# Retention and two MoE layers on one core: half of the first token chunk moved into a short pass between the seven-product passes, clamp of weight words moved to VectorE

## The chip, the cores and the metric

The kernel runs on one core of a Trainium2 chip. The metric is the device time of one execution in microseconds. Five engines work side by side: TensorE (PE for its matmuls, PEld for its weight loads), VectorE (DVE), ScalarE (ACT), GpSimd (POOL), and SyncE (SP), which here issues all the DMAs. Each works through its own instructions in the order in which they were written into the program.

## What is computed

```python
def _attn_ref(q, k, v):            # 4 batches, 8 heads, 576 positions, 64 dims
    scores = scale * np.matmul(q, k.transpose(0, 1, 3, 2))
    Dmat = np.where(rel >= 0, gamma[:, None, None] ** rel[None, :, :], 0.0)
    return np.matmul(scores * Dmat, v)

def _moe_ref(x, w_gate, w_val, w_out):      # 2304 tokens, 512 wide, 1536 hidden
    g = x @ w_gate
    silu = g * (1.0 / (1.0 + np.exp(-g)))
    return silu * (x @ w_val) @ w_out

def _moe2_ref(x, w_in, w_out):              # 2048 hidden
    r = np.maximum(x @ w_in, 0.0)
    return (r * r) @ w_out
```

The output of the retention is `x` of the first layer, and the output of the first layer is `x` of the second. The weights of both layers arrive as 64-bit floating-point numbers and are made into 32-bit ones on the chip. The matmuls run on a pair of reduced-precision parts (`hi` and `lo`) of each operand: every product of two 32-bit operands is three matmuls (`three`, L312): hi by hi, hi by lo, lo by hi.

## The kernel before, in words

**Tiles.** The activations live in `xy`, a tile of 128 partitions by four channel blocks by 2304 tokens. The hidden width is cut into units of 128 rows: 12 of them (`F1`) in the first layer, 16 (`F2`) in the second. A weight *unit* is a 128x512 block: gate ("g"), value ("v") or output ("o") of one hidden block in the first layer, input ("i") or output ("o") in the second. That makes 36 units of the first layer and 32 of the second.

**Conversion of a unit** (`words` L163, driven by `conversion` L191 and `conversion2` L261). A DMA brings 512 KB of 64-bit words into a `raw` tile. Two ScalarE instructions take out the low bits and the magnitude, one instruction clamps the magnitude (L175, on GpSimd: `pool_e.tensor_scalar` with max and min), and three instructions of VectorE shift and mask, put the sign in, and add the low bits. The result is stored to DRAM (`wst`). For the first layer, `parts_unit` (L155) also makes the hi and lo parts at once (one ScalarE copy, one VectorE subtraction). The raw tiles come from a pool of two (`raw_p`), and for part of the time from places in `xy` that are not in use yet (`spare`). The generators yield between the steps; `pump` and `pump2` run so many steps between other pieces of work.

**Order of the work.** Four stages follow each other.

1. Retention, 16 pairs of heads in a loop of 18 turns (L510 on), with an order that is written by hand: while `chain["on"]` holds, each instruction is placed behind the one before it on its engine. In turns 6 to 17 each turn also does one projection of the *first chunk* (the first `M0` = 512 tokens): gate and value of the hidden units 0 to 5, four channel blocks by three matmuls. Fourteen units are converted alongside.
2. The rest of the first chunk (L777 to L805): the output matmuls `out0` (L352) of units 0 to 5, and gate, value and output of units 6 to 11, for which the other 22 units of the first layer are converted. All twelve output contributions add up in four PSUM banks, and the sum is then copied into `xy`. `renew` (L569) of the next pass and `build(0)` are interleaved with the last seven steps.
3. Two *seven-product passes* over the other 1792 tokens (L827 on). Each takes two blocks of 448 tokens; for a pair of hidden units the four block products of 2x2 blocks of weights and activations are made from seven products of sums and differences (Strassen's method in Winograd's form). A *system* is one pair of hidden units for gate or value: seven *slots* of six matmuls. `renew` makes the seven activation operands (four subtractions on GpSimd, then a hi and lo split on ScalarE and VectorE), `stationary` (L241) makes the weight operands on GpSimd with splits, in the first of the passes only; they are stored (`win`) and loaded again in the second. `out1` (L723) then does the output matmuls of the pair into a PSUM bank, and adds them to `xy`. The second layer's units are converted during these passes, with `PACE` steps per slot.
4. Three such passes over all 2304 tokens with blocks of 384 for the second layer, and the DMA of the output.

Outside the chained loop of stage 1 a planner orders the instructions: it goes through a simulated time line and takes, for each engine, the first instruction in program order that is ready then; so a step of a conversion that stands late in the program can be placed early where an engine is free, and how far ahead is limited by the raw tiles and the tiles that it writes.

The operands of a slot come from here:

```python
    ROWS = ((1, 2), (6, 3), (7, 4), (5,))          # which products share a weight tile
    for x in ((1, n), (7, n - 1), 0, (2, n), (4, n - 1), 1, (6, n), (3, n - 1), 2, (5, n)):
        # (i, k): slot i of system k;  0, 1, 2: a third of the due output tiles
```

Of the kernel before, what the change touches and what calls it, by code (L numbers as in the profile page):

```python
# [9 lines left out]
F32 = mybir.dt.float32  # L10
# [37 lines left out]
PUMPS = {0: 1, "E": 2, "out": 4}  # L48

PACE = (0.3, 1.9)  # L50
# [9 lines left out]
def retention_moe_kernel(  # L60
# [19 lines left out]
    raw_p = pool(ctx, "raw_p", 2)  # L80
    cv_p = pool(ctx, "cv_p", 1)
    ph1 = ExitStack()
    ctx.enter_context(ph1)
    xs_p = pool(ph1, "xs_p", 4)
    h_p = pool(ph1, "h_p", 2)
    t_p = pool(ph1, "t_p", 2)
    wa_p = pool(ph1, "wa_p", WA)
# [42 lines left out]
    def prefetch(upto):  # L130

        while loads["next"] <= min(upto, len(order) - 1):
# [11 lines left out]
            what, f = order[i]  # L144
            src = w1[f, :, "gvo".index(what), :].bitcast(U32)
# [4 lines left out]
    wst = {(1, *u): part_p.tile([P, 512], F32, tag=f"w1{u[0]}{u[1]}", name="wst") for u in order}  # L150
# [4 lines left out]
    def parts_unit(i):  # L155
        wf = w_t.pop(i).bitcast(F32)
        hi, lo = weight_tiles()
        act.copy(hi, wf)
        dve.tensor_tensor(out=lo, in0=wf, in1=f32(hi), op=ALU.subtract)
        sp.dma_start(out=wst[(1, *order[i])], in_=wf)  # L160
        units[order[i]] = (hi, lo)

    def words(raw, back, flat):  # L163
# [11 lines left out]
        pool_e.tensor_scalar(out=wf, in0=wf, scalar1=TINY, scalar2=HUGE, op0=ALU.max, op1=ALU.min)  # L175
# [15 lines left out]
    def conversion():  # L191
        for i in range(len(order)):
            prefetch(max(i, min(i + 3, loads["cap"])))
            raw, back = raw_t[i]
            for n, wt in enumerate(words(raw, back, raw_flat.pop(i, None))):
                w_t[i] = wt
                if n == 2:
                    if i:
                        parts_unit(i - 1)
                else:  # L200
                    yield
# [6 lines left out]
        parts_unit(len(order) - 1)  # L208
        yield


    seq2 = [(what, f) for f in range(F2) for what in "io"]
    wst.update({(2, *u): part_p.tile([P, 512], F32, tag=f"w2{u[0]}{u[1]}", name="wst") for u in seq2})
    raw2, free2, count = {}, [None, None], {"load2": 0}

    def load2(upto):
        while count["load2"] < len(seq2) and count["load2"] <= upto and free2:
            j = count["load2"]
            count["load2"] += 1
            back = free2.pop(0)  # L220
            flat = None
            if back is None:
                flat = raw_p.tile([P, 1024], U32, tag="raw", name="raw")
                raw = flat.rearrange("p (a n) -> p a n", a=2)
            else:
                raw = back.bitcast(U32)
            what, f = seq2[j]
            src = w2[f, :, "io".index(what), :].bitcast(U32)
            sp.dma_start(out=raw, in_=src.rearrange("p (a n) -> p a n", a=2))
            raw2[j] = raw, back, flat  # L230

    def give_back(j):
        back = raw2.pop(j)[1]
        if back is None or loads["open"]:
            free2.append(back)
# [25 lines left out]
    def conversion2():  # L261
        behind = None
        for j, u in enumerate(seq2):
            load2(j + 2)
            for n, wt in enumerate(words(*raw2[j])):
                if n == 3 and behind is not None:
                    sp.dma_start(out=behind[0], in_=behind[1])
                if n != 2:
                    yield
            give_back(j)  # L270
            behind = wst[(2, *u)], wt.bitcast(F32)
        sp.dma_start(out=behind[0], in_=behind[1])
        yield

    pumped = {"n": 0, "limit": 0}
    convert = conversion()
    convert2 = conversion2()

    def pump2(k=1):
        for _ in range(k):  # L280
            next(convert2, None)
# [7 lines left out]
    def ensure(key):  # L289
        while key not in units:  # L290
            next(convert)
            pumped["n"] += 1
# [28 lines left out]
    def project(f, what):  # L321
        ensure((what, f))
        ps, w = bank(what), units.pop((what, f))
        for cc in range(CC):
            three(ps, cut(w, cc * P, P), xs[cc], cc == 0, cc == CC - 1)
        return ps
# [3 lines left out]
    def hidden0(k):  # L330
# [11 lines left out]
        if f < HALF:  # L342
            hi, lo = weight_tiles()
        else:
            hi = h_p.tile([P, M0], F32R, tag="hh", name="h_hi")
            lo = h_p.tile([P, M0], F32R, tag="hl", name="h_lo")
# [3 lines left out]
    acc = []  # L350

    def out0(f):  # L352

        if f == 0:
            acc.extend(ps_a.tile([P, 512], F32, tag=f"a{i}", name=f"a{i}") for i in range(CC))
        ensure(("o", f))
        w, h = units.pop(("o", f)), hs.pop(f)
        for cc in range(CC):
            three(acc[cc], cut(w, cc * P, P), h, f == 0, f == F1 - 1)
        if f == F1 - 1:  # L360
            for cc, a in enumerate(acc):
# [553 lines left out]
```

## Time and profile before

| | us |
|---|---|
| median of three runs (lowest, highest) | 950.38 (950.35, 951.18) |
| the profiled execution | 946.6 |
| its span in the trace | 944.8 |
| busy: PE, PEld | 897.1, 780.6 |
| busy: DVE, ACT, POOL | 668.2, 435.8, 283.8 |

The span is the time from the first to the last instruction that the trace holds; what the execution's own time has beyond it lies around it. Busy time of PE is modelled: the end of a pipelined matmul is not recorded, so that two matmuls in flight overlap and a busy PE can still take fewer matmuls than it could. The number of matmuls in a stretch, (x...) in the views, tells more. Every instruction of this kernel is recorded at the line of the helper that issues it, so groups are told apart by the names of the tiles: `g`, `v`, `z` are PSUM tiles of projections, `oacc` of output matmuls, `a` of the first chunk's output; `xo` the activation operands and `wi` the weight operands of the seven products; `raw`, `w` the conversion; `w_hi`, `w_lo` split units.

### The profile page before, as it was taken

The page shows a single profiled execution, that of the slowest core. Times are in us where ns is not written, and L with a number is a line of the kernel's source. Part 1 is how long each engine was busy: PE and PEld are TensorE (multiplying, and loading weights), DVE is VectorE, ACT ScalarE, POOL GpSimd, SP SyncE. Part 2 cuts the span into 40 slices and gives each one's busy share as a digit, 9 for nine tenths or more (in the row PEclk, how much of TensorE's full clock was granted, in tenths as well). Part 3 has the DMA queues.
Part 4 walks back from the last instruction along what each step waited for, and adds up shares of the span by engine and source line. Part 5 has one row for each costly group of instructions (what it writes and reads, how often), then busy time and mean ns, then how long its engine had stood idle before and what let it go on. Part 6 is the DMA issues. An engine that isn't in the chain of part 4 may idle for free.

```text
span 944.8 us, 13815 instructions
## 1 busy us (share of the span) xinstructions
PE 897.1 (95%) x5050; PEld 780.6 (83%) x5050; DVE 668.2 (71%) x1011; ACT 435.8 (46%) x780; POOL 283.8 (30%) x207
## 2 busy tenths in 40 slices
PE   7899977777999999999999999999999999999998
PEld 6777745555899899799999998898989889989986
DVE  4777687778989999986545798767754557554553
ACT  3655645544775566635323545544423334243220
POOL 2544474565565653643000263310200002000000
PEclk9999989998999999999999999999999999999999
DMA  9988496653798889779445446455464544564402
GB/s 331 338 281 272 141 329 218 175 172 134 249 319 315 313 289 350 247 244 321 152 152 156 151 183 233 166 181 184 139 198 149 188 138 152 167 212 145 131 26 67
DMA packets 80660, 196.30 MB, mean 208 GB/s; under 512 B 8144, under 2 KB 18896, under 8 KB 80592
## 3 DMA queue, kind: packets, MB, share of 16 engines
q1 hardware_dynamic: 80592, 195.41, 61.9%
q8 instruction: 40, 0.66, 0.3%
q14 instruction: 28, 0.23, 0.1%
HBM read 136.14 MB, written 59.24 MB: 207 GB/s over the span
## 4 chain that ended last, share of the span: by engine, by line
PE 68%; DVE 11%; DMA 9%; issue 5%; POOL 3%; ACT 3%; SPq 0%; POOLq 0%; DVEq 0%; ACTq 0%
PE oacc L112 28%; PE g L112 19%; PE v L112 10%; DVE w L112 5%; PE z L112 5%; DMA raw<-in_w 4%; PE o L112 3%; PE s L112 2%; POOL w L112 2%; DMA xy<-in_w 2%; DVE wi L112 1%; DVE xy L112 1%; DMA qk_sb<-in_qk 1%; PE kvs L112 1%; DVE ho_lo L112 1%
## 5 line engine op out<-in xcount | busy, mean ns | idle before, releaser
L112 PE MATMUL g<-xo_h,wi 128*128 128x384 f32 (+1 forms) x768 | 232.1, 353 | 6.0 <-ACT cai L112 2.9
L112 POOL TENSOR_SCALAR w<-w 128x512 f32<-128x512 f32 x68 | 143.3, 2108 | 139.7 <-ACT w L112 123.3
L112 PE MATMUL oacc<-wo,ho_hi 128*128 128x512 f32 x576 | 181.8, 393 | 0.0
L112 PEld LDWEIGHTS g<-xo_h,wi 128*128 128x128 f32 x768 | 143.0, 188 | 17.4 <-ACT cai L112 3.6
L112 PE MATMUL g<-xo_l,wi 128*128 128x384 f32 (+1 forms) x384 | 135.1, 352 | 0.0
L112 PEld LDWEIGHTS oacc<-wo,ho_hi 128*128 128x128 f32 x576 | 107.6, 188 | 18.4
L112 PE MATMUL v<-xo_h,wi 128*128 128x448 f32 (+1 forms) x384 | 121.4, 355 | 1.3 <-DVE t L112 1.0
L112 PE MATMUL oacc<-ho_hi,wo 128*128 128x448 f32 x384 | 120.8, 366 | 0.0
L112 DVE TENSOR_TENSOR xy<-oacc,xy 128x448 f32<-128x448 f32 (+1 forms) x134 | 85.4, 644 | 39.7 <-PE oacc L112 39.4
L112 PE MATMUL oacc<-wo,ho_lo 128*128 128x512 f32 x288 | 113.4, 394 | 0.0
L112 POOL TENSOR_TENSOR xy<-xy 128x768 f32<-128x768 f32 (+1 forms) x20 | 44.0, 2212 | 160.9 <-DVE xo_l L112 160.6
L112 PEld LDWEIGHTS v<-xo_h,wi 128*128 128x128 f32 x384 | 72.2, 190 | 8.0 <-DVE t L112 1.4
L112 PEld LDWEIGHTS oacc<-ho_hi,wo 128*128 128x128 f32 x384 | 72.1, 188 | 6.3
L112 PEld LDWEIGHTS g<-xo_l,wi 128*128 128x128 f32 x384 | 72.2, 188 | 5.2
L112 PE MATMUL oacc<-ho_lo,wo 128*128 128x448 f32 x192 | 70.2, 366 | 0.0
L112 PE MATMUL v<-xo_l,wi 128*128 128x448 f32 (+1 forms) x192 | 67.8, 353 | 0.0
L112 ACT ACTIVATE raw<-raw 128x512 uint32<-128x512 uint16 x58 | 39.4, 680 | 58.8 <-DMA raw<-in_w 57.2
L112 DVE TENSOR_TENSOR wo<-wo 128x512 fp32r<-128x512 f32 x72 | 49.3, 703 | 22.7 <-ACT wo L112 22.6
L112 PE MATMUL z<-xo_h,wi 128*128 128x448 f32 (+1 forms) x192 | 60.3, 352 | 3.8 <-ACT xy L112 2.9
L112 PEld LDWEIGHTS oacc<-wo,ho_lo 128*128 128x128 f32 x288 | 54.0, 188 | 11.2
L112 ACT CAST wo<-wo 128x512 fp32r<-128x512 f32 x72 | 43.3, 620 | 34.2 <-DMA wo<-wst 33.4
L112 DVE TENSOR_SCALAR w<-w 128x512 uint32<-128x512 uint32 x68 | 44.0, 648 | 20.3 <-POOL w L112 20.0
(118 smaller groups left out, 1587.4 us busy)
## 6 DMA issues: line engine op xcount, KB each, us to landing
wi<-win SPq DMA_DIRECT2D x84, 512.0 KB, 3.7
win<-wi SPq DMA_DIRECT2D x60, 512.0 KB, 4.7
raw<-in_w SPq DMA_DIRECT2D x58, 512.0 KB, 4.5
wo<-wst SPq DMA_DIRECT2D x72, 256.0 KB, 4.3
wst<-w SPq DMA_DIRECT2D x68, 256.0 KB, 4.6
w_in<-wst SPq DMA_DIRECT2D x40, 256.0 KB, 4.9
qk_sb<-in_qk SPq DMA_DIRECT2D x15, 576.0 KB, 6.0
kv_sb<-in_kv SPq DMA_DIRECT2D x15, 576.0 KB, 4.7
```

Of the source, the lines that this page charges most:

```text
L112: i = op(*args, **kw)
```

## The change

The first chunk is made shorter, 448 tokens for 512, and the blocks of the two passes of the first layer longer, 464 for 448. Only the hidden units 0 to 5 of the first chunk are still done at the start: their output sum is copied out of PSUM through two `raw` tiles and stored to a DRAM tile (`part`). The units 6 to 11 of the first chunk become a pass of their own, "rest", of six plain systems (k = 3, 4, 5 by gate and value) between the two seven-product passes. It uses the weight units loaded again from `wst`, the operand tiles and buffers of the passes, and adds its output to `xy`, into which `part` has been loaded. System 0 of the first seven-product pass is interleaved with the six `out0` (`seq` at n == 0). All 68 units are now converted in one sequence; the first 18 get their hi and lo parts at once, the other 50 are only stored. The steps are paced at 1.1 per slot. `ensure` makes a load wait until its unit has been stored in program order. The clamp and the four subtractions of `renew` go from GpSimd to VectorE.

```diff
-M0 = 512
-M = {1: 448, 2: 384}
+M0 = 448
+M = {1: 464, 2: 384}
 TOKENS = {
-    1: [(M0 + M[1], M0 + 2 * M[1]), (M0, M0 + 3 * M[1])],
-    2: [(M[2] * p, NT // 2 + M[2] * p) for p in range(NT // (2 * M[2]))],
+    (1, 0): (M0 + M[1], M0 + 2 * M[1]),
+    (1, "rest"): (0,),
+    (1, 1): (M0, M0 + 3 * M[1]),
+    **{(2, p): (M[2] * p, NT // 2 + M[2] * p) for p in range(NT // (2 * M[2]))},
 }
...
-PUMPS = {0: 1, "E": 2, "out": 4}
-
-PACE = (0.3, 1.9)
+PUMPS = {0: 1, "out": 4}
+
+PACE = 1.1
...
-    order = [(what, f) for f in range(HALF) for what in "gv"] + [("o", 0), ("o", 1)]
-    order += [x for f in range(HALF, F1) for x in (("g", f), ("v", f), ("o", f - HALF + 2))]
-    order += [("o", f) for f in range(F1 - HALF + 2, F1)]
+    order = [(1, what, f) for f in range(HALF) for what in "gv"] + [(1, "o", f) for f in range(HALF)]
+    plain = len(order)
+    for k in range(HALF // 2, F1 // 2):
+        order += [(1, what, f) for f in (2 * k, 2 * k + 1) for what in "gv"] + [(1, "o", 2 * k), (1, "o", 2 * k + 1)]
+    for k in range(F2 // 2):
+        order += [(2, what, f) for what in "io" for f in (2 * k, 2 * k + 1)]
...
-    def parts_unit(i):
+    def finish(i):
         wf = w_t.pop(i).bitcast(F32)
-        hi, lo = weight_tiles()
-        act.copy(hi, wf)
-        dve.tensor_tensor(out=lo, in0=wf, in1=f32(hi), op=ALU.subtract)
-        sp.dma_start(out=wst[(1, *order[i])], in_=wf)
-        units[order[i]] = (hi, lo)
+        if i < plain:
+            hi, lo = weight_tiles()
+            split(hi, lo, wf)
+            units[order[i]] = (hi, lo)
+        sp.dma_start(out=wst[order[i]], in_=wf)
+        stored.add(order[i])
...
-        pool_e.tensor_scalar(out=wf, in0=wf, scalar1=TINY, scalar2=HUGE, op0=ALU.max, op1=ALU.min)
+        ts(out=wf, in0=wf, scalar1=TINY, scalar2=HUGE, op0=ALU.max, op1=ALU.min)
...
     def out0(f):
...
+        for cc, a in enumerate(acc):
+            if cc % 2 == 0:
+                o = raw_p.tile([P, 1024], U32, tag="raw", name="part_sb").bitcast(F32)
+            dst = o[:, (cc % 2) * 512:][:, :M0]
+            act.copy(dst, a)
+            sp.dma_start(out=part[:, cc, :], in_=dst)
...
     def renew(at, i):
...
-        if i == 5:
-            pool_e.tensor_tensor(out=b12, in0=b12, in1=b11, op=ALU.subtract)
...
+            if i == 5:
+                tt(out=b12, in0=b12, in1=b11, op=ALU.subtract)
...
     def build(n):
...
+        if p == "rest":
+            to(0, w0)
+            for _ in range(5):
+                yield
+            to(2, w1_)
+            return
...
+    def plain_slot(n, r):
+
+        ph, p, k, what = systems[n]
+        ps = bank("gv"[r])[:, :M0]
+        product(n, ps, True, *(((1, 1), (2, 2)), ((7, 1), (4, 2)))[r])
+        if what == "g":
+            if r == 0:
+                sys_[n] = {"a": temp("ag", 2)[:, :, :M0]}
+            act.activation(out=sys_[n]["a"][:, r], in_=ps, func=AF.Silu)
+            return
+        ga = sys_[n - 1]["a"]
+        tt(out=ga[:, r], in0=ps, in1=ga[:, r], op=ALU.mult)
+        if r:
+            hidden(n, "a", ga)
...
+            seq = [("out", 0), ("out", 1), (1, n), ("out", 2), (5, n), ("out", 3), (6, n), ("out", 4), ("out", 5), (2, n)]
+            for i in (1, 5, 6, 2):
+                renew(passes[0], i)
...
+        if (n, p) == (systems.index((1, "rest", HALF // 2, "g")) + 1, "rest"):
+            sp.dma_start(out=xy[:, :, :M0], in_=part)
...
-            if 0 < n < flip - 1:
-                pace["due"] += PACE[n >= F1]
-                pump2(int(pace["due"]))
-                pace["due"] %= 1
+                if n < flip - 1:
+                    pace["due"] += PACE
+                    pump(int(pace["due"]))
+                    pace["due"] %= 1
```

## Rows read from the trace of the kernel before

**Rows 1.** The page: busy time of each engine over the span

```profile
PE 897.1 (95%) x5050; PEld 780.6 (83%) x5050; DVE 668.2 (71%) x1011; ACT 435.8 (46%) x780; POOL 283.8 (30%) x207
```

**Rows 2.** Busy time by stretch: start:end, length, engines (instructions), clock, DMA share, GB/s

```profile
0.00:119.00 119.00, 111.24 (x1306) 87.87 (x1307) 78.23 (x154) 62.32 (x139) 50.55 (x53) 1.00 0.81 273
119.00:240.00 121.00, 91.50 (x335) 65.42 (x334) 97.37 (x139) 63.19 (x108) 71.50 (x40) 0.92 0.62 198
240.00:410.00 170.00, 166.89 (x810) 151.02 (x809) 160.65 (x236) 103.70 (x181) 93.77 (x66) 1.00 0.85 298
410.00:535.00 125.00, 124.98 (x612) 114.48 (x611) 74.78 (x114) 51.22 (x89) 19.78 (x12) 1.00 0.62 201
535.00:610.00 75.00, 72.03 (x360) 66.10 (x359) 63.09 (x90) 37.75 (x67) 32.41 (x27) 0.98 0.54 192
...
940.50:944.80 4.30, 0.00 (x0) 0.00 (x0) 0.68 (x1) 0.00 (x0) 0.00 (x0) 0.97 0.23 68
```

**Rows 3.** Waits of PEld from 119 to 240: us in total, times, longest

```profile
PEld g L112 <- ACT w_hi L112: 12.1, 6, 3.6
PEld a L112 <- ACT w_hi L112: 7.1, 6, 2.0
```

**Rows 4.** The chain that ended last: start us, us, what

```profile
54.31 2.94 PE g L112 x12
...
447.04 2.43 PE g L112 x12
...
680.27 2.77 PE oacc L112 x12
...
693.80 2.08 PE g L112 x12
```

**Rows 5.** Instructions that write or read w: shortest, median, longest ns, first to last start

```profile
L112 POOL TENSOR_SCALAR w<-w x68: 1908/2004/3542, 27.4 to 444.4; 128x512 f32<-128x512 f32 x68
L112 DVE TENSOR_SCALAR w<-w x68: 408/427/2343, 29.4 to 446.3; 128x512 uint32<-128x512 uint32 x68
...
L112 DVE CUSTOM_DVE_ANT_0 w<-raw,w x62: 412/681/2510, 32.6 to 448.8; 128x1024 uint16<-128x1024 uint16 x54, 128x512 uint16<-128x512 uint16 x8
L112 ACT ACTIVATE w<-raw x58: 639/662/697, 26.6 to 443.7; 128x512 f32<-128x512 f32 x58
L112 DVE SCALAR_TENSOR_TENSOR w<-raw,w x58: 674/686/2477, 30.6 to 447.7; 128x512 uint32<-128x512 uint32 x58
...
L112 DVE TENSOR_TENSOR w_lo<-w,w_hi x36: 674/692/2582, 35.2 to 229.7; 128x512 fp32r<-128x512 f32 x36
```

**Rows 6.** Groups by shape over the span: busy us, mean ns, idle before

```profile
L112 DVE TENSOR_TENSOR xy<-oacc,xy 128x448 f32<-128x448 f32 x80 | 48.3, 614 | 4.5 <-PE oacc L112 4.3
L112 DVE TENSOR_TENSOR wi<-w_in,wi 128x512 fp32r<-128x512 f32 x60 | 47.4, 796 | 6.1 <-ACT wi L112 6.0
...
L112 DVE TENSOR_SCALAR w<-w 128x512 uint32<-128x512 uint32 x68 | 44.0, 648 | 20.3 <-POOL w L112 20.0
...
L112 POOL TENSOR_TENSOR xy<-xy 128x896 f32<-128x896 f32 x8 | 19.4, 2436 | 1.7 <-DVE xo_l L112 1.5
...
L112 DVE TENSOR_TENSOR xo_l<-xy,xo_h 128x896 fp32r<-128x896 f32 x14 | 15.3, 1093 | 4.8 <-ACT xo_h L112 4.8
```

**Rows 7.** Instructions on raw from 240 to 410: the second conversion in the first pass

```profile
L112 DVE SCALAR_TENSOR_TENSOR w<-raw,w x24: 674/685/2477, 240.0 to 406.2; 128x512 uint32<-128x512 uint32 x24
```

**Rows 8.** DMA issues: queue, count, KB each, median us from issue to landing

```profile
raw<-in_w SPq DMA_DIRECT2D x58, 512.0 KB, 4.5
wo<-wst SPq DMA_DIRECT2D x72, 256.0 KB, 4.3
...
w_in<-wst SPq DMA_DIRECT2D x40, 256.0 KB, 4.9
```

**Rows 9.** Waits over the span: us in total, times, longest

```profile
POOL w L112 <- ACT w L112: 123.3, 49, 9.8
...
ACT raw L112 <- DMA raw<-in_w: 57.2, 36, 2.9
```

More of the change, by code (lines that the diff above doesn't have):

```diff
@@ L207, in conversion @@
             yield
-        parts_unit(len(order) - 1)
+        finish(len(order) - 1)
         yield
[L212 to L235, printed above, removed]
     def split(hi, lo, src):
@@ L321, in project @@
     def project(f, what):
[L322 to L323 removed]
+        ensure((1, what, f), units)
+        ps, w = bank(what)[:, :M0], units.pop((1, what, f))
         for cc in range(CC):
@@ L341, in hidden0 @@
         yield
[L342 to L346, printed above, removed]
+        hi, lo = (x[:, :M0] for x in weight_tiles())
         split(hi, lo, t)
@@ L544, in retention_moe_kernel @@
         pump(PUMPS[0])
-        assert loads["next"] == UNITS_EARLY and not raw_t
+        assert loads["next"] == UNITS_EARLY and not raw_t and not loads["pool"]
         loads["cap"], loads["open"] = len(order) - 1, False
@@ L557, in retention_moe_kernel @@
     tt = dve.tensor_tensor
-    systems = [(1, p, k, what) for p in range(len(TOKENS[1])) for k in range(F1 // 2) for what in "gv"]
-    systems += [(2, p, k, "i") for p in range(len(TOKENS[2])) for k in range(F2 // 2)]
+    passes = list(TOKENS)
+    systems = [
+        (ph, p, k, what)
+        for ph, p in passes
+        for k in range(HALF // 2 if p == "rest" else 0, (F1, F2)[ph - 1] // 2)
+        for what in ("gv", "i")[ph - 1]
+    ]
     win = {
@@ L766, in retention_moe_kernel, with after @@
             fetch.setdefault(n + 1, []).append((ph, range(2 * k - 2, 2 * k + 2)))
+    def after(n, i):
+        at = systems[n][:2]
+        if n + 1 == len(systems) or systems[n + 1][:2] == at or at == passes[-1]:
+            return
+        nxt = passes[passes.index(at) + 1]
+        if at[1] == "rest":
+            for x in (1, 2) if i == "s1" else ():
+                renew(nxt, x)
+        elif nxt[1] == "rest" and i not in (1, 2):
+            nxt = (1, 1)
+        if at[1] != "rest" and i != 6:
+            for x in (5, 6) if i == 5 else (i,):
+                renew(nxt, x)
@@ L832, in retention_moe_kernel @@
             i, k = x
+            if i == "out":
+                out0(k)
+                pump(PUMPS["out"])
+                if k > 2:
+                    renew(passes[0], {3: 7, 4: 4, 5: 3}[k])
+                if k == HALF - 1:
+                    parts.close()
+                    ho_p = pool(mid, "ho_p", 2)
+                    wo_p = pool(mid, "wo_p", 4)
+                continue
             if n == flip + 1 and i == 4:
@@ L836, in retention_moe_kernel @@
                 wo_p = pool(ctx, "wo2_p", 8)
[L837 removed]
+            if 0 <= k < end and systems[k][1] != "rest":
                 slot(k, i)
+            elif i in ("s0", "s1"):
+                plain_slot(k, int(i[1]))
+            else:
+                k = end
             next(make, None)
[L840 to L850 removed]
+            if k < end:
+                if n < flip - 1:
+                    pace["due"] += PACE
+                    pump(int(pace["due"]))
+                    pace["due"] %= 1
+                after(k, i)
+        for _ in make:
+            pass
         if n == flip - 1:
[L852 removed]
+            for _ in convert:
                 pass
```

223 lines of the change are left out of this document (93 added, 130 removed).

## The prediction, made before the changed kernel was run

> **What bounds the kernel now.** I read the page's busy line first [rows 1]. TensorE leads with 95% of the span, VectorE has 71%, GpSimd 30%. That would leave TensorE little to gain, but it is a mean over four stages, so I cut the span at the stages [rows 2]. Look at the count of matmuls beside the length: 810 in 170 us and 612 in 125 us where the seven-product passes run, but 335 in the 121 us between 119 and 240, which is the rest of the first chunk. In that stretch VectorE is busy 97.4 and GpSimd 71.5 us. The waits of the weight loads there say what is late [rows 3]: the hi parts of weight units, 12.1 us for the projections and 7.1 us for the outputs. The conversion of 22 units sets the pace, and TensorE waits for it.
>
> To turn counts into work I take TensorE's cadence from the chain, where twelve matmuls follow each other without a gap [rows 4]: 448 columns 2.43/12 = 0.2025 us, 512 columns 2.77/12 = 0.2308, 384 columns 2.08/12 = 0.1733. From 384 to 512 that is 0.00045 us a column, so 464 columns take 0.2025 + 16 x 0.00045 = 0.2097 (an estimate). By the code the stretch from 119 to 240 holds 288 matmuls of 512 columns; the other 47 have 448. That is 288 x 0.2308 + 47 x 0.2025 = 76.0 us of work in 121, so 45.0 us idle. From 240 to 410: 810 x 0.2025 = 164.0, 6.0 idle. From 410 to 535: 123.9, 1.1 idle.
>
> The Trainium skill (Perfetto Trace Analysis, Identifying the Most-Contended Engine) warns that matmul occupancy is a poor measure, and takes the share of weight loads. By matmul busy time [rows 2] the stretch would have 121 - 91.5 = 29.5 us idle, and the forecast would come out 15.5 us later, at 934.5. By weight loads, with 114.48/125 = 0.916 as a full engine, it has 121 - 65.4/0.916 = 49.6, and the forecast would be 4.6 us earlier.
>
> The whole first layer after 119 has 1584 x 0.2025 + 288 x 0.2308 = 387.3 us of work, the second layer 1008 x 0.1733 + 864 x 0.2308 = 374.1, and 4.3 us follow the last matmul [rows 2]. So 944.8 - 119 - 387.3 - 374.1 - 4.3 = 60.1 us are idle after 119, of which 60.1 - 45.0 - 6.0 - 1.1 = 8.0 come after 535, about the change to the second layer.
>
> **The change, part by part.**
>
> *Columns.* The chained stage has 144 projection matmuls with 448 columns for 512: 144 x 0.0283 = 4.1 us less. TensorE sets that stage, as [rows 4] shows for one of its projections, so it ends at 114.9. Bounds: 0, if the conversion that is chained beside it holds it, and 4.1. Then come 1584 x 0.2097 + 288 x 0.2025 = 390.5 us for the first layer, 3.2 more than now. Nearly nothing is won in work; what can be won is idle time.
>
> *Conversions out of TensorE's way.* Before the passes only four units (output 2 to 5) are left to convert instead of 22. The other 50 go beside the passes, where TensorE has stored work. So the 45.0 us go, and what a start with four units costs comes in their place.
>
> *The clamp.* 68 GpSimd instructions of 2.0 us go, 68 VectorE instructions come. VectorE's mask of the same shape, also with one tile in and out, takes 0.427 (median) [rows 5]; that is the nearest row, and I take it. The lower end is its shortest, 0.408, and the upper the clamp's own 2.0 on GpSimd. 54 lie after the chained stage: 23 us. Their cover is VectorE's free time, below. The 14 in the chained stage, 6 us, lie in its 119 - 78 = 41 us free [rows 2].
>
> *The four subtractions of renew.* They take 2.4 us each on GpSimd [rows 6]; on VectorE the nearest is the lo split of the same width, 1.09 [rows 6]. Three passes have them after 115: 12 x 1.09 = 13 us. From below I allow 0.6, the add of 448 columns, from above 2.4. GpSimd is left with the weight sums and what they wait for.
>
> *VectorE's total.* It had 97.4 + 160.7 + 74.8 = 332.9 us of work from 119 to 535 [rows 2]. Add 23 and 13, and 12 output adds of the rest pass at 0.614 [rows 6], 7 us, and about 3 for wider blocks. Splits for parts fall away and come again at other places (18 units no longer split, 12 + 6 split after loading again): nothing. Take away the delays that GpSimd's clamp causes: the mask takes 0.648 in the mean [rows 6] against 0.427, so 0.22 x 54 = 12 us; the bounds are 0 and about twice that, since other instructions have such long cases too. Sum 367 us, in a stretch from 115 to about 518: 91%. In the first pass VectorE is at 160.7/170 = 95% now, with 24 units converted beside it [rows 7], and TensorE lost 6.0 us. So the passes bear it: 24 units in the first pass, few in the rest pass, and 22 in the second, where VectorE now has 125 - 75 = 50 us free and needs 22 x 2.2 = 49. If the clamp took 2.0, the sum would be 367 + 85 = 452 us and VectorE would be the bound.
>
> *The start of the passes.* VectorE's work: four units at 0.427 + 0.427 + 0.686 + 0.681 + 0.692 [rows 5], 11.7 us; 7 splits and 4 subtractions of renew, 11 x 1.09 x 464/448 = 12.4; the weight parts of systems 0 and 1, 2 x 3.5 x 0.796 [rows 6] = 5.6; and some five smaller ones, 3. Together 32.7, against 72 x 0.2025 + 42 x 0.2097 = 23.4 us on TensorE. VectorE overhangs by 9.3, and the first loads must land; I take 12 idle. Lower end: the raw tiles alone. A turn is 4.5 for landing [rows 8], 1.3 on ScalarE, 2.2 on VectorE, 8.0 with two tiles, so the fourth unit is ready at 114.9 + 8 + 3 x 4 + 1.3 = 136, its output ends at 138.6, and TensorE had 14.6 + 3.8 of work by then: 5 idle. Upper end: only two outputs (4.9 us) run under the 32.7, 28 idle. The copy of the sum frees the bank that product 2 writes: a ScalarE instruction (0.66 for 512 columns [rows 5]), in this 12. The stores of the sum also hold both raw tiles, and the raw loads stand behind them on SP's queue: one turn of conversion, 8 us, hidden as long as conversions are ahead of use.
>
> *The rest pass.* 144 + 72 matmuls, counted above. VectorE has about 40 us in its 44 (splits of loaded weights, 7 operands for the next pass), so I take 4 idle; 1 to 10. Loads: 12 + 6 of 256 KB and the sum out and in, 6.4 MB, at 298 GB/s [rows 2] 21 us of transfer in a stretch whose DMAs were at 0.62. They are issued a system ahead, 13 us against 4.9 landing [rows 8]; 0 on the path, and 5 each if the lead is lost. SP's queue gets 23 issues more.
>
> *Sum.* 114.9 + 390.5 + 374.1 + 4.3 = 883.8. Idle: start 12, first pass 5 (now 6.0), rest 4, second pass 2 (now 1.1; it now converts throughout), second layer 7 (now 8.0; its renew no longer waits for GpSimd). That is 30, so the span is 913.8, 31.0 less. The profiled execution's own time, 946.6, is 1.8 above its span and 3.8 under the median 950.38; the same steps give 915.6 and, for the median, 919.
>
> **The rivals.**
>
> *VectorE's queue holds the clamp* (slower). GpSimd stood 123.3 us in 49 waits for the ScalarE step ahead of the clamp [rows 9], 2.5 us each, and nobody was behind it. On VectorE everything is behind it. At W us for each of 54 units VectorE needs 367 + 54 W; the time equals today's where 114.9 + T + 374.1 + 4.3 + 7 = 944.8, T = 444.5, W = 1.44. At 2.0 the stretch is 475 and the median 950 + 30 = 980. For it: ScalarE itself waits 57.2 us in 36 times for the raw loads, 1.6 each [rows 9]. Against: an engine with nothing else arrives early and waits long; a full one arrives late, and the mask behind the clamp waits 20.0 us in 68 now [rows 6], 0.3 each. The Trainium skill (TensorE: Matmul & The Clock Gate, Architectural detail) says that VectorE's queue is strictly first in, first out; by that rule each such wait holds all behind it, and no row here shows it directly. Chance 0.08.
>
> *VectorE is late in several places, but not all the time*: start 20, first pass 8, rest 9, second 5, second layer 8: 50 idle, median 939. For it: 95% in the first pass already. Chance 0.21.
>
> *The start is covered*: 5, 3, 2, 1, 6: 17 idle, median 906. For it: GpSimd's long stays are gone. Chance 0.11.
>
> *The change doesn't do what it says*: the planner places the later conversions ahead of system 0's operands, and TensorE waits for units as now: start 45, the others as forecast, 63 idle, median 952. Against: program order favours system 0. Chance 0.05.
>
> **How the numbers follow.** The forecast, 919, has 0.55; with the bounds of its terms it reaches from 908 to 932. The range 904 to 942 takes in the two rivals about it, most of the way; left out are the slower ends and the far edges, 0.2. A measurement of this kernel can tell 0.2%, 1.9 us. Faster: 0.55 + 0.21 + 0.11 = 0.87. Slower: 0.08 + 0.02. Same: 0.03, the rest of the last rival.
>
> **What would show it.** Right: 119 to 240 has over 530 matmuls; clamps of about 0.43 us; VectorE over 90% up to 500; the first matmul of the second layer near 515; the chain runs over TensorE through the first pass. Wrong: waits of VectorE's clamp for ScalarE beyond 1 us a unit, clamps of 0.65 or more, TensorE idle over 20 us from 115 to 150, or second-layer conversions still running after 520 with the passes waiting for them.

## The result, and the profile after

The changed kernel took 917.97 us (median of 4 runs, 916.48 to 920.45) against 950.37 for the kernel before: ratio 0.966, 95% interval 0.9634 to 0.9686. The forecast was 919. The profiled execution took 920.45 us, with a span of 918.7; it is the slowest of the four and stands 2.5 over their median, and the table below shows where it lost about that much. The profiled execution before stands 3.8 under its median, so the spans differ by 26.1 us where the medians differ by 32.4.

The page's line of busy times after, which answers to [rows 1]:

```profile
PE 884.8 (96%) x5050; PEld 782.0 (85%) x5050; DVE 679.3 (74%) x1098; ACT 438.6 (48%) x781; POOL 103.3 (11%) x119
```

GpSimd lost 180 us of work and VectorE gained only 11, although it has 87 instructions more. Part of that is the new order, which gives and takes VectorE's work too. The kernel below with the new order and both moves undone has 669.0 us on VectorE, so that the 88 moved instructions add 10.3. Why so little, the experiments explain.

Busy time by stretch after, with the columns of [rows 2]:

```profile
118.50:240.00 121.50, 107.19 (x482) 92.92 (x482) 105.56 (x165) 74.29 (x135) 39.43 (x34) 0.93 0.82 282
240.00:410.00 170.00, 164.93 (x782) 147.06 (x781) 151.48 (x249) 94.94 (x158) 14.67 (x17) 0.99 0.80 267
410.00:520.00 110.00, 109.36 (x522) 97.61 (x521) 87.67 (x148) 55.77 (x94) 4.77 (x6) 1.00 0.76 261
520.00:610.00 90.00, 89.83 (x458) 82.44 (x458) 74.62 (x111) 47.24 (x85) 22.50 (x24) 1.00 0.56 202
...
```

Read the counts first: 482 matmuls in the stretch after the chained stage, where [rows 2] had 335. Three marks on TensorE's timeline cut the span more sharply: the first chained projection, the end of the chained stage, and the first matmul of 384 columns, with which the second layer begins. Before (start, us, what):

```profile
39.70 0.50 PE L112 MATMUL g<-xh,w_hi 128*128 128x512 f32 x1
...
119.12 0.39 PE L112 MATMUL a<-w_hi 128*128 128x512 f32 x1
...
541.42 0.34 PE L112 MATMUL g<-xo_h,wi 128*128 128x384 f32 x1
```

After:

```profile
42.44 0.47 PE L116 MATMUL g<-xh,w_hi 128*128 128x448 f32 x1
...
118.19 0.36 PE L116 MATMUL v<-xh,w_lo 128*128 128x448 f32 x1
...
520.23 0.33 PE L116 MATMUL g<-xo_h,wi 128*128 128x384 f32 x1
```

The same marks of the experiments, in profiled executions, give this table (us; the end of the chained stage is the start of its last matmul plus one cadence of 0.20, and before it is the first output matmul, which follows without a gap):

| kernel | ahead of the chained stage | chained stage | from there to the second layer | second layer to the end | span |
|---|---|---|---|---|---|
| before | 39.7 | 79.4 | 422.3 | 403.4 | 944.8 |
| after | 42.4 | 76.0 | 401.8 | 398.5 | 918.7 |
| clamp back on GpSimd | 39.6 | 75.9 | 408.4 | 398.0 | 921.9 |
| subtractions back on GpSimd | 41.4 | 76.1 | 415.0 | 400.6 | 933.1 |
| both back | 40.9 | 76.9 | 413.2 | 401.5 | 932.6 |
| first sums on VectorE | 39.6 | 75.9 | 394.7 | 398.3 | 908.5 |

So 20.5 us came out of the stretch from the chained stage to the second layer, 4.9 out of the second layer and 3.4 out of the chained stage; 2.7 were lost ahead of it, where the granted clock was 0.91 up to 40 us. That last loss is no part of the change: the kernel of the last line has the same work there and began at 39.6.

### The profile page after: what moved, and what is told of

Its sections match the earlier page's. It is cut to its first block, busy times and chain, and to the rows that moved or that the text cites. A ratio compares the mean times of both kernels' runs of the same rounds, so it can differ in the third digit from the quotient of the medians.

```text
span 918.7 us, 13809 instructions
## 1 busy us (share of the span) xinstructions
PE 884.8 (96%) x5050; PEld 782.0 (85%) x5050; DVE 679.3 (74%) x1098; ACT 438.6 (48%) x781; POOL 103.3 (11%) x119
## 4 chain that ended last, share of the span: by engine, by line
PE 71%; DMA 11%; DVE 10%; issue 3%; ACT 3%; POOL 1%; SPq 1%; ACTq 0%; DVEq 0%; POOLq 0%
PE oacc L116 29%; PE g L116 20%; PE v L116 11%; DMA raw<-in_w 6%; PE z L116 4%; DVE w L116 3%; PE o L116 3%; PE s L116 3%; DVE wi L116 2%; DMA w_in<-wst 1%; DVE xy L116 1%; DMA wst<-w 1%; DMA win<-wi 1%; DVE xo_l L116 1%; DMA kv_sb<-in_kv 1%
## 5 line engine op out<-in xcount | busy, mean ns | idle before, releaser
L116 PE MATMUL g<-xo_h,wi 128*128 128x464 f32 (+2 forms) x816 | 251.1, 359 | 9.4 <-ACT wi L116 3.3
L116 PE MATMUL g<-xo_l,wi 128*128 128x464 f32 (+2 forms) x408 | 146.1, 358 | 0.0
L116 PE MATMUL v<-xo_h,wi 128*128 128x464 f32 (+2 forms) x432 | 136.8, 359 | 7.9 <-ACT wi L116 5.3
L116 PE MATMUL oacc<-ho_hi,wo 128*128 128x464 f32 (+1 forms) x432 | 138.5, 372 | 0.5 <-DVE xy L116 0.5
L116 DVE TENSOR_TENSOR xy<-oacc,xy 128x464 f32<-128x464 f32 (+2 forms) x146 | 94.3, 650 | 33.8 <-PE oacc L116 33.6
L116 PEld LDWEIGHTS oacc<-ho_hi,wo 128*128 128x128 f32 x432 | 81.0, 188 | 10.1 <-DVE xy L116 0.9
L116 DVE TENSOR_SCALAR w<-w 128x512 f32<-128x512 f32 (+1 forms) x136 | 58.6, 431 | 37.2 <-ACT w L116 36.4
L116 PE MATMUL oacc<-ho_lo,wo 128*128 128x464 f32 (+1 forms) x216 | 80.1, 371 | 0.0
L116 PE MATMUL v<-xo_l,wi 128*128 128x464 f32 (+2 forms) x216 | 77.2, 357 | 0.0
L116 ACT CAST wi<-w_in 128x512 fp32r<-128x512 f32 x72 | 44.1, 618 | 38.2 <-POOL w_in L116 9.2
L116 PE MATMUL z<-xo_h,wi 128*128 128x464 f32 (+1 forms) x192 | 61.8, 360 | 0.2 <-DVE cag L116 0.2
```

The source lines that it names most:

```text
L116: i = op(*args, **kw)
```

## The experiments

**One part undone at a time.** Each ratio below is to runs of the kernel before that were taken beside the same experiment. Its median there was 947.83, 949.31, 947.12 or 947.42 us, against 950.37 beside the kernel after, so ratios are compared across experiments, and where the plain times say something else, that is given too. The next three kernels share their runs of the kernel before.

The clamp back on GpSimd:

```diff
-        ts(out=wf, in0=wf, scalar1=TINY, scalar2=HUGE, op0=ALU.max, op1=ALU.min)
+        pool_e.tensor_scalar(out=wf, in0=wf, scalar1=TINY, scalar2=HUGE, op0=ALU.max, op1=ALU.min)
```

> The changed kernel with the clamp back on GpSimd (one line). Theory A (the move of the clamp unloads: GpSimd's 2 us clamps lengthen each conversion and make VectorE's own instructions longer): 6 to 14 us slower than the changed kernel, about 924 to 932, with VectorE's mask at a mean of 0.6 us or more again. Theory B (the two engines share access to memory, and every instruction moved to VectorE holds up GpSimd's weight sums, which the start waits for): the same or up to 6 us faster, 912 to 918, and the wait of the first weight operand shorter.

Measured: 924.64 us, ratio 0.9761 (0.9741 to 0.9781).

The four subtractions of `renew` back on GpSimd:

```diff
-                tt(out=b12, in0=b12, in1=b11, op=ALU.subtract)
+                pool_e.tensor_tensor(out=b12, in0=b12, in1=b11, op=ALU.subtract)
...
```

> The changed kernel with the four subtractions of renew back on GpSimd. Theory A: 2 to 8 us slower (920 to 926), since each renew then has a step of over 2 us in its chain at the start and at the change to the second layer; the idle time after 520 goes from under 1 to some 5 us. Theory B: 2 to 6 us faster (912 to 916), since VectorE has 4 us less in the burst at the start, in which one GpSimd sum took 5.4 us.

Measured: 932.27 us, ratio 0.9844 (0.9818 to 0.9869), slower than either expectation.

Both back, which leaves the new order and the new sizes alone:

> The changed kernel with clamp and subtractions both on GpSimd: new order and new block sizes alone. Theory A: the order brings most of the gain, 45 us of waiting for units go, but the start and the passes cost 10 to 20 us more than in the changed kernel: 928 to 938. Theory C (the order alone is worth little, the clamp on VectorE is what makes room): 940 to 952.

Measured: 934.76 us, ratio 0.9872 (0.9849 to 0.9895).

Put on the 950.4 us of the kernel before, the order and sizes alone give 12 us. On that base the subtractions give 10.5 more, or 17.5 if the clamp has moved already; the clamp gives 2.6, or 9.6 if the subtractions have. Each alone adds up to 25, together they give 32: while either stays on GpSimd, part of the other's gain is held back. How much is less sure. By the plain times the subtractions give 10.1 or 14.3 and the clamp 2.5 or 6.7, so that 4 us are held back instead of 7. Either way the subtractions, which the forecast took for an added load, are worth about as much as the new order and sizes, and more once the clamp has moved.

Why they are worth so much is plain on VectorE's timeline of the kernel with the subtractions back, at the start of the passes (start us, us, what). GpSimd:

```profile
127.33 7.29 POOL L116 TENSOR_TENSOR xy<-xy 128x928 f32<-128x928 f32 x3
```

and VectorE in the same 7 us:

```profile
127.58 2.38 DVE L116 TENSOR_SCALAR w<-w 128x512 uint32<-128x512 uint32 x1
129.88 2.69 DVE L116 TENSOR_TENSOR wi<-w_in,wi 128x512 fp32r<-128x512 f32 x1
132.49 3.11 DVE L116 TENSOR_TENSOR xo_l<-xy,xo_h 128x928 fp32r<-128x928 f32 x1
135.53 1.21 DVE L116 TENSOR_TENSOR w_lo<-w,w_hi 128x512 fp32r<-128x512 f32 x1
```

One VectorE instruction to each GpSimd subtraction, and each some 2 us longer than alone: the mask of a conversion 2.38 for 0.43, the split of a weight operand 2.69 for 0.68, the split of an activation operand 3.11 for 1.1. VectorE is shown as busy, but it is waiting inside its instructions. The Trainium skill (SBUF — State Buffer, SBUF: two separate sides) says that the port pair which VectorE and GpSimd share goes to one instruction as a whole and is not divided; these three rows agree.

The page's busy lines of that kernel, and of the one with the clamp back, give the whole price:

```profile
PE 893.5 (96%) x5050; PEld 784.9 (84%) x5050; DVE 685.6 (73%) x1078; ACT 437.5 (47%) x781; POOL 148.1 (16%) x139
```

```profile
PE 888.2 (96%) x5050; PEld 783.1 (85%) x5050; DVE 667.2 (72%) x1030; ACT 438.2 (48%) x781; POOL 244.2 (26%) x187
```

After has the 20 subtractions on VectorE, in these groups (by shape: busy us, mean ns, idle before):

```profile
L116 DVE TENSOR_TENSOR xy<-xy 128x768 f32<-128x768 f32 x12 | 11.6, 997 | 0.1
L116 DVE TENSOR_TENSOR xy<-xy 128x928 f32<-128x928 f32 x6 | 7.2, 1204 | 0.1
L116 DVE TENSOR_TENSOR cbv<-xy 128x928 f32<-128x928 f32 x2 | 2.2, 1116 | 0.0
```

They take 21.0 us there. With them gone from VectorE its busy time is 685.6, not 679.3 - 21.0 = 658.3: its other instructions took 27.3 us longer. The subtractions cost VectorE more on GpSimd than on VectorE itself. With the clamp back, VectorE has 667.2 for 679.3 - 29.6 = 649.7, so 17.5 of the clamp's 29.6 us come back as delays.

In time, each subtraction is also a step of the chain at a change of pass. On GpSimd (by shape, subtractions back) one of 928 columns takes twice the 1.2 us of after, and GpSimd stands waiting for VectorE's splits before it:

```profile
L116 POOL TENSOR_TENSOR xy<-xy 128x928 f32<-128x928 f32 x6 | 14.1, 2360 | 21.4 <-DVE xo_l L116 15.2 <-ACT xy L116 6.1
```

In the windows of that kernel the loss lies in the stretches that hold changes of pass:

```profile
240.00:410.00 170.00, 158.29 (x740) 138.34 (x739) 152.88 (x246) 89.84 (x153) 25.16 (x21) 0.99 0.78 259
...
520.00:600.00 80.00, 77.91 (x396) 71.40 (x395) 66.22 (x95) 42.41 (x76) 35.42 (x29) 1.00 0.53 188
```

740 matmuls for 782 after; and from 520 to 600 TensorE stands for 2.1 of 80 us, where after is full. The counts there, 396 and 409, differ mostly because this kernel enters the second layer, with its shorter matmuls, only at 532.5:

```profile
520.00:600.00 80.00, 79.83 (x409) 73.42 (x409) 68.66 (x103) 43.88 (x79) 22.50 (x24) 1.00 0.59 211
```

**One part alone.** The clamp on VectorE in the old order:

```diff
-        pool_e.tensor_scalar(out=wf, in0=wf, scalar1=TINY, scalar2=HUGE, op0=ALU.max, op1=ALU.min)
+        ts(out=wf, in0=wf, scalar1=TINY, scalar2=HUGE, op0=ALU.max, op1=ALU.min)
```

> The kernel before with the clamp on VectorE (one line). Theory A: the stretch from 119 to 240 waits for conversions, whose chain gets some 1.5 us shorter for each of 22 units, part of it on the path: 5 to 15 us faster, 935 to 945. Theory C: most of the gain is in this line: 920 to 930. Theory D (VectorE, 97 of 121 us busy there, is the limit, and gets 9 us more): 950 to 956.

Measured: 942.87 us, ratio 0.9966 (0.9945 to 0.9987), some 3 us by the ratio and 5 by the medians. In the 121 us behind its chained stage, which ends at 122.2, it had 360 matmuls for the 334 of the kernel before, but its subtractions were still on GpSimd. So the clamp by itself is not what the change lives on. The subtractions alone on VectorE in the old order were not run.

The new sizes in the old order:

```diff
-M0 = 512
-M = {1: 448, 2: 384}
+M0 = 448
+M = {1: 464, 2: 384}
...
```

> The kernel before with a first chunk of 448 and blocks of 464, everything else as it was. (Two spare places for raw words reach 64 tokens into the next block, whose activations they overwrite; the amount of work is the same.) All theories: 4.1 us less in the chained stage and 4 to 8 us less work in the stretch up to 240, which is waiting time anyway, 3 to 11 us more in the passes: within 4 us of the kernel before, 944 to 954.

Measured: 955.77 us, ratio 1.0066 (1.0047 to 1.0085), 6 us slower, just beyond the expectation. Since two places for raw words overwrite activations, as the expectation says, its output is not the reference's: it stands for the time of this amount of work alone. Its stretch after the chained stage still waits for conversions (25 us of the weight loads' waits there are for hi parts of units):

```profile
119.00:240.00 121.00, 85.09 (x332) 68.06 (x331) 98.89 (x140) 63.30 (x109) 72.09 (x40) 0.87 0.63 197
```

332 matmuls, so shorter blocks without the new order buy nothing there, and the passes pay for 464 columns. With the 12 us of order and sizes together, the order is worth 18 on top of the sizes; the order with the old sizes was not run.

**What holds the start of the passes.** After, TensorE still idles there, by count 121.5 - 100.3 = 21 us up to 240 (73 matmuls of 448 columns at 0.2025, the last of the chained stage among them, and 409 of 464 at 0.209), and all of it before 180. Three windows after:

```profile
118.50:180.00 61.50, 47.19 (x196) 39.25 (x196) 51.46 (x75) 35.45 (x66) 21.96 (x17) 0.86 0.77 256
120.00:140.00 20.00, 11.17 (x39) 7.85 (x40) 18.56 (x24) 9.66 (x19) 14.17 (x9) 0.76 0.54 196
...
180.00:280.00 100.00, 100.00 (x478) 89.31 (x477) 89.10 (x151) 60.78 (x108) 26.05 (x27) 1.00 0.85 294
```

39 matmuls of about 0.207 us leave 12 of the 20 us idle, and VectorE is busy for 18.56 of them. A loss by count is not all standing still. From 118.5 to 180 TensorE is busy for 47.19 of 61.5 us, so it stands for 14.3; in the other 7 it starts anew and works slowly. After a wait of 5.27 us its matmuls of 464 columns started 0.39 us apart, for 0.209, the lower of the clock's two levels, and the granted clock is 0.76 from 120 to 140 and 0.86 from 118.5 to 180 (timeline):

```profile
134.25 0.76 PE L116 MATMUL v<-xo_h,wi 128*128 128x464 f32 x1 [5.27 <-ACT wi L116]
...
137.88 0.59 PE L116 MATMUL v<-xo_l,wi 128*128 128x464 f32 x1
138.27 0.59 PE L116 MATMUL v<-xo_h,wi 128*128 128x464 f32 x1
```

The 45.0 us of the kernel before are of the same kind: it stands for 121 - 91.5 = 29.5 of them, and its granted clock there is 0.92 [rows 2]. The weight loads' waits from 112 to 182 after:

```profile
PEld v L116 <- ACT wi L116: 5.7, 1, 5.7
PEld g L116 <- ACT wi L116: 3.7, 1, 3.7
PEld v L116 <- DVE wi L116: 3.6, 2, 2.2
```

In the timeline a weight sum of GpSimd, 0.77 us in the median of its 20, took 5.36, and ended at 130.65, shortly before VectorE's next gap. An earlier one is shown with it:

```profile
118.20 1.48 POOL L116 TENSOR_TENSOR s<-w_in 128x256 f32<-128x256 f32 x1 [15.43 <-DMA w_in<-wst]
...
125.29 5.36 POOL L116 TENSOR_TENSOR w_in<-s,w_in 128x256 f32<-128x256 f32 x1 [4.03 <-DVE wi L116]
```

VectorE's gaps about it (one row to a gap, in brackets what ended it):

```profile
116.93 3.73 DVE L116 TENSOR_TENSOR xo_l<-xy,xo_h 128x928 fp32r<-128x928 f32 x3 [1.49 <-ACT xo_h L116]
...
132.19 0.69 DVE L116 TENSOR_TENSOR wi<-w_in,wi 128x512 fp32r<-128x512 f32 x1 [1.26 <-ACT wi L116]
```

From 116.93 to 132.19 - 1.26 = 130.93 it had none. Two causes fit: the held-up sum, or VectorE's own backlog. The first system's sums on VectorE tell them apart:

```diff
...
-        for _ in stationary(w0, w1_, s1, to):
+        for _ in stationary(w0, w1_, s1, to, (pool_e if n else dve).tensor_tensor):
```

> The changed kernel with the four weight sums of system 0 on VectorE instead of GpSimd. Theory B (a GpSimd instruction that reads two tiles gets no turn while VectorE runs two-tile instructions back to back, so the 5.4 us of one sum stood on the path of the start): the wait of 5.3 us ahead of product 3 of system 0 shrinks to 1 to 2 us and the time falls by 3 to 6 us, 912 to 915. Theory E (VectorE's backlog sets the start, as the prediction had it; the sums add 2 us to it): 0 to 3 us slower, 918 to 921.

Measured: 910.19 us, ratio 0.9592 (0.9572 to 0.9613). It has the lowest median of all the kernels, below both expectations, but the window from 120 to 140 again holds 39 matmuls. Its chained stage ends 2.9 us earlier; counted from that end, 121.6 us lose 18.8 us where after loses 21.3. The hold-up moved to the next system's sum, and TensorE waited behind it; in the order of time, GpSimd, ScalarE and TensorE:

```profile
127.59 4.83 POOL L116 TENSOR_TENSOR s<-w_in 128x256 f32<-128x256 f32 x1 [27.72 <-DVE w_in L116]
...
132.46 0.41 ACT L116 CAST wi<-s 128x256 fp32r<-128x256 f32 x1 [5.17 <-POOL s L116]
132.92 0.75 PE L116 MATMUL v<-xo_h,wi 128*128 128x464 f32 x1 [8.57 <-ACT wi L116]
```

So the sums of the second system went to VectorE too (the edit against the kernel with the first sums):

```diff
-        for _ in stationary(w0, w1_, s1, to, (pool_e if n else dve).tensor_tensor):
+        for _ in stationary(w0, w1_, s1, to, (pool_e if n > 1 else dve).tensor_tensor):
```

> The changed kernel with the weight sums of systems 0 and 1 on VectorE. With system 0's alone the gain came, but not where it was expected: TensorE still had 11.9 us idle from 120 to 140, since system 1's first sum on GpSimd then took 4.8 us, and ScalarE's split of system 0 stood behind it. Theory B (held-up GpSimd sums set the start): with none left there, idle from 120 to 140 falls to 4 to 7 us, 904 to 909. Theory H (VectorE's backlog sets the start, whoever does the sums): idle stays at 10 to 13 us, 909 to 916.

Measured: 911.61 us, ratio 0.9621 (0.9576 to 0.9667). With hardly any GpSimd work there (window), VectorE still had no gap from 115.3 to 137.8, and TensorE waited (window and timeline):

```profile
120.00:140.00 20.00, 11.94 (x49) 9.88 (x48) 19.70 (x36) 10.67 (x18) 1.41 (x1) 0.83 0.59 189
```

```profile
115.28 3.20 DVE L116 TENSOR_TENSOR xo_l<-xy,xo_h 128x928 fp32r<-128x928 f32 x3 [1.47 <-ACT xo_h L116]
...
133.46 0.74 PE L116 MATMUL a<-w_hi 128*128 128x448 f32 x1 [7.87 <-ACT w_hi L116]
...
138.07 0.59 DVE L116 TENSOR_SCALAR w<-w 128x512 f32<-128x512 f32 x1 [0.30 <-ACT w L116]
```

From the end of its chained stage 18.0 us are lost, so the held-up sums are worth 3 of the 21 us at most, and the time came out as the expectation with the backlog had it. That the backlog is the rest of the cause follows by exclusion. Two runs tried to work on it. The first system's weights ahead of the other operands on VectorE's queue (on top of the first sums):

```diff
...
-            for _ in build(0):
+            renew(passes[0], 1)
+            first = build(0)
+            for _ in range(4):
+                next(first)
+            with tc.issue_after(dve.seen):
+                for i in (5, 6, 2):
+                    renew(passes[0], i)
+            for _ in first:
...
```

> As the run before, and the renew of products 5, 6 and 2 of system 0 placed behind the first system's first weight split on VectorE. Theory F (the start waits for the weight operands, whose splits stood in VectorE's queue behind five instructions of renew): 3 to 6 us below the run before, 907 to 912, and TensorE idle under 15 us from 118 to 180. Theory E: the same as the run before, within 2 us, since the backlog is only put in another order.

Measured: 913.06 us, ratio 0.9608 (0.9588 to 0.9628), no better than without it. Its start did lose less, 16.9 us from the end of the chained stage for 18.8, but the 170 us from 238.3 on have 778 matmuls where the kernel with the first sums has 812, in a profiled execution that is the slowest of its six. And four units more converted in the chained stage:

```diff
-UNITS_EARLY = 14
+UNITS_EARLY = 18
...
-            fill = PUMPS[0] if n >= FROM - 2 else 0
+            fill = PUMPS[0] * (1 + (n >= last - 1)) if n >= FROM - 2 else 0
```

> The changed kernel with 18 units converted in the chained stage instead of 14: the last four turns of its loop run twice as many steps, so that no conversion is left for the start of the passes. Theory H (VectorE's backlog sets the start, 14 us without a gap there): 11.7 us of VectorE's work leave the burst, the idle time from the first output matmul to 180 falls from 19 to 8 us or less, and the chained stage gets 0 to 4 us longer: 906 to 913. Theory J (the start waits for the first weight operands and their loads whatever else VectorE does): idle stays above 14 us, 916 to 922.

Measured: 915.93 us, ratio 0.9665 (0.9634 to 0.9697), the time of after, and nearest to the expectation that doubts the backlog. Windows and TensorE's timeline:

```profile
120.00:140.00 20.00, 10.30 (x47) 8.98 (x48) 19.93 (x31) 13.34 (x21) 0.00 (x0) 0.74 0.38 118
140.00:180.00 40.00, 38.41 (x181) 33.14 (x180) 35.02 (x52) 25.98 (x48) 17.25 (x18) 1.00 1.00 366
```

```profile
132.93 0.74 PE L116 MATMUL a<-w_hi 128*128 128x448 f32 x1 [9.52 <-ACT xy L116]
```

The idle time from 140 to 180 goes almost wholly, as the other expectation had it, but the first output starts 13 us later: the chained stage takes 81.5 us for 76.0, and TensorE then waits 9.52 us for a ScalarE copy that stands behind conversions and splits in ScalarE's queue. What the start saves, the chained stage and that wait take. So the work was moved and not saved, which fits a backlog of VectorE and ScalarE together but doesn't prove it. This edit with the first sums on VectorE:

> The run before with the weight sums of system 0 on VectorE, as in the fastest run so far. Theory H: 900 to 908. Theory J: 908 to 913.

Measured: 913.84 us, ratio 0.964 (0.961 to 0.967): nothing beyond the first sums alone, and slower than both expectations.

**Where the gain of the first sums comes from.** It is 7.8 us by the medians and 6.5 by the ratios. 2.5 come from the start, as counted above, and most comes from 240 to 410 (window):

```profile
240.00:410.00 170.00, 169.40 (x812) 151.74 (x811) 151.82 (x256) 94.88 (x160) 11.86 (x12) 1.00 0.82 276
```

812 matmuls for 782, 30 x 0.209 = 6.3 us: next to nothing is idle at the changes of pass. The largest single piece that after loses there is in ScalarE's queue, as its timeline shows:

```profile
381.53 0.65 ACT L116 ACTIVATE raw<-raw 128x512 uint32<-128x512 uint16 x1 [3.83 <-DMA raw<-in_w]
...
382.64 0.52 ACT L116 COPY cbg<-g 128x464 f32<-128x464 f32 x1
...
383.21 0.76 PE L116 MATMUL g<-xo_h,wi 128*128 128x464 f32 x1 [2.61 <-ACT cbg L116]
```

ScalarE stood 3.83 us for a raw load, and the copy that frees TensorE's bank was queued behind it. Why one system's sums change what the queue meets 250 us later is argued only: the planner's order shifts with the costs. To see what one other shift of that kind makes, the pace of the conversions was changed alone:

```diff
-PACE = 1.1
+PACE = 1.2
```

> The changed kernel with 1.2 conversion steps a slot instead of 1.1, to see how far the planner's order alone moves the time. Theory A (VectorE has room for the conversions wherever they stand): within 2 us of the changed kernel, 916 to 920. Theory G (the gain hangs on this pace): over 4 us slower or faster.

Measured: 917.72 us, ratio 0.9664 (0.9637 to 0.9691), no difference. And whether VectorE can take all the sums:

```diff
...
-        for _ in stationary(w0, w1_, s1, to):
+        for _ in stationary(w0, w1_, s1, to, dve.tensor_tensor):
```

> The changed kernel with all weight sums of both layers on VectorE; GpSimd then works in the chained stage only. VectorE gets 80 instructions of 0.42 us, 34 us. Theory B: no GpSimd instruction is held up and none lengthens VectorE's: 900 to 908. Theory I (VectorE has no room left in the first pass, 34 us more make it the bound there): 920 to 935.

Measured: 927.37 us, ratio 0.9788 (0.9751 to 0.9825), slower than after by 12 us (9 by the medians), and much of the loss is in the passes:

```profile
240.00:410.00 170.00, 162.61 (x756) 142.73 (x755) 151.44 (x266) 92.82 (x154) 0.00 (x0) 0.98 0.79 262
```

So GpSimd's one remaining job, the later weight sums, is well placed. That VectorE has no room for them, as the expectation said, is not shown: it is as busy there as after (151.44 us for 151.48) while TensorE does 26 matmuls less, and TensorE's longest wait is for a ScalarE copy again (3.3 us). Why the planner's order comes out better with just the first sums moved stays open.

## Why the prediction was right, and where its terms were off

*The total.* 919 against 917.97. The bound was named rightly: 45 us of idle TensorE in the rest of the first chunk, waiting for conversions. After, 21 are idle up to 240. From 240 to 520, 216 x 0.2025 + 1088 x 0.209 = 271 of 280, so 9. From 520 to the tail at 914.6, 86 x 0.209 + 374.1 = 392.1 of 394.6, so 2.5. Together some 32; the forecast was 30. All these are losses by count, standing and lower clock together.

*Luck in the last step.* The forecast's span is 913.8 and the profiled one 918.7, mostly because the chained stage ended at 118.4 for 114.9. The step from the span to the median then added 3.8 us, because the profiled execution before stood that far under its median. The one after stands 2.5 over, so that step had no ground in this kernel, and it makes up for the span. That 919 lies within 1 us of 917.97 is luck; a gain of about 30 us is not.

*Cadences and columns.* Confirmed. Twelve matmuls of 464 columns take 2.51 us in after's chain, 0.209 each for the estimated 0.2097, and the chained stage is 3.4 us shorter for 4.1:

```profile
402.76 2.51 PE g L116 x12
```

*The clamp.* Confirmed as a price. By shape, after:

```profile
L116 DVE TENSOR_SCALAR w<-w 128x512 f32<-128x512 f32 x68 | 29.6, 435 | 36.7 <-ACT w L116 36.4
L116 DVE TENSOR_SCALAR w<-w 128x512 uint32<-128x512 uint32 x68 | 29.1, 427 | 0.5
```

0.435 against 0.427, and the mask went from the 0.648 of [rows 6] to 0.427, the whole of the delay that was taken away. But the step put that delay down to GpSimd's clamp alone, and this was the wrong cause for its longest cases: the longest mask is 2.34 us before [rows 5] and 2.4 wherever the subtractions are on GpSimd, and 0.96 with the clamp alone there. The longest belong to the subtractions. Of the mean both have a share: moving the clamp alone in the old order took it from 0.648 to 0.527.

*The subtractions.* This is the term that failed. The step added 13 us to VectorE and put at nothing what they did to VectorE's other instructions from GpSimd. The runs show that VectorE's load falls by 6 when they come to it (679.3 for 685.6), and that they are worth 10.5 to 17.5 us of time. *VectorE's total* was too high: 367 us by 518, against 105.56 + 151.48 + 87.67 = 345 by 520. The kernels between the marks of the table show the steps: from the end of the chained stage to the second layer VectorE has 339.2 us before, 338.5 with the new order and both moves undone, and 344.8 after. So the order added nothing where 10 were forecast, and the two moves 6 where 24 were.

*The start.* Forecast 12 idle, up to 28; measured about 21. The mechanism was right as far as the runs show it (VectorE overhangs TensorE), the size was not. TensorE stands for 14.3 us, near the forecast; the other 7 are restarts and matmuls at the lower clock after its waits, for which the step had no term. It also weighed 32.7 us of VectorE's work as a whole against the matmuls, and TensorE stands for the single operand that is late; that the order of the work matters there is argued, with the 2 us that the start won by the first weights ahead for it.

*The second layer.* Forecast 7 idle, measured 2.5. The step said that its `renew` no longer waits for GpSimd, and still credited 1 of 8; with both parts back on GpSimd 3.0 of the 4.9 us come back in the table, 2.1 with the subtractions alone. The first, rest and second passes were forecast at 11 together, and 9 are measured from 240. So a start that cost 9 more and passes and a second layer that cost 6 less nearly cancel, which is why the sum of the idle terms came out so close; this too is luck.

*The rivals.* The clamp in VectorE's queue fell. Of after's waits:

```profile
ACT raw L116 <- DMA raw<-in_w: 62.8, 36, 5.9
...
DVE w L116 <- ACT w L116: 36.4, 26, 3.4
```

36.4 us over 68 units are 0.54 each, and the rival needed 1.44. Its mechanism exists, though, on ScalarE: the copy behind the raw load at 381.5. VectorE late in several places, 939, was too dear. The covered start, 906, is not what happened, but the kernel with the first sums on VectorE comes near it by full passes instead of a full start.

*Signs.* "Over 530 matmuls from 119 to 240" was missed: 482 from 118.5. VectorE over 90% up to 500 was missed too: 87% up to 240, 89% to 410, 80% to 520, because its load was put too high. "The chain runs over TensorE through the first pass" was missed as well: from 201 to 282 it runs over conversions and DMAs, though TensorE is full up to 280. The second layer began at 520.23 for 515, 2.7 of that from the late start of the profiled execution. Of the signs that would have made it wrong none came: the clamps' waits are 0.54 us a unit, the clamps take 0.435 us, the second layer's conversions are done by 492, and from 115 to 150 TensorE is busy for 24.7 of 35 us, so it stands for 10 us, and loses 14 by count, where over 20 were named.

## What to carry to other kernels

An engine's busy time can hold another engine's work: if instructions of one shape have a long tail, look at what runs beside the long ones, and price a move by what those get back. Undo parts singly and together, since parts that share a resource need not add up (together they gave 4 to 7 us more here than singly). And gauge TensorE by matmuls times cadence, stretch by stretch: it found the 45 us that busy shares hid. Then set the busy time and the granted clock beside it, since such a loss is part standing and part slow work.

## What the runs showed of the hardware that was not expected

A subtraction of two 928-column tiles on GpSimd holds VectorE's instruction beside it about 2 us, whether that has one input tile (the mask, 2.38 for 0.43) or two (the split, 3.11 for 1.1). The other way about it can be worse: weight sums of GpSimd of 0.74 to 0.77 us (medians) took 5.36 and 4.83 us while VectorE issued without a gap. The second ended inside VectorE's next gap; the first ended at 130.65, beside an addition of VectorE that reads a PSUM tile (from 129.98 to 130.59) and the clamp behind it. For over 4 us GpSimd got no turn between VectorE's instructions.

That is not a rule. The sum at 118.20 took 1.48 us while VectorE issued without a gap too, and there VectorE's three splits from 116.93 on took 3.73 us, for 3.20 in the kernel where GpSimd had nothing to do beside them. Which of the two happens, and whether an instruction with a PSUM input is what lets GpSimd in, no run here settles.
